# Recurrent steps on single buffers, with two fewer streamed weight blocks and a new order of the matmul units

## The chip, the cores and the metric

The kernel runs on one core of a Trainium2 chip. The metric is the time of the whole kernel on the device, in microseconds, as the median of three runs. The profile is one further execution, taken by the hardware profiler.

## The reference

Two branches work on the same input `x` (2048 tokens of 640 numbers, bf16) and a gate mixes them.

```
g = sigmoid((x * gate_w).sum(-1))          # one number per token
a = sliding-window attention of x          # 32 heads of 20, each token sees the last 256
b = recurrent memory transformer of x      # below
out = g * a + (1 - g) * b

mem = mem0                                 # 8 rows of 640
for s in range(64):                        # segments of 32 tokens
    h = concat(mem, x[32*s : 32*s+32])     # 40 rows
    q, k, v = h @ Wq, h @ Wk, h @ Wv       # 32 heads of 192
    p = softmax(mask(q k^T / sqrt(192)))   # memory rows see all; a token sees no later row
    o = (p v) @ Wo                         # back to 640
    mem = o[:8]; emit o[8:]                # the next step needs these 8 rows
```

The recurrence is strict: step s+1 cannot start its projections before the memory rows of step s exist.

## The kernel before

**Stages.** First comes the sliding-window branch (`branch_A`). Its output, already multiplied by g, is written to `ga_dram`. Then a dense stage computes q, k and v for the last 8 tokens of every segment, all segments at once, since these rows hold no memory. Its results go to the DRAM tensor `xin`, beside the transposed input of each segment. Then `branch_B` runs the 64 recurrent steps on the other 32 rows (8 memory rows and 24 tokens); most of the time is spent there.

**One step.** The 32 heads are worked on in 4 groups g of 8. Each step is a list of units for TensorE (PE), written out by hand in `STEP`, and the same list is issued for every step:

- `k`, `q`, `v` followed by g: a projection of the group, 20 matmuls over 5 slices of the 640 inputs (L772). ScalarE (ACT) copies the result out of PSUM into `tok` or `vtok` (L783).
- `tk`, `tq`: the transposes of k and q (L796). VectorE (DVE) writes k into the buffers `K02` (shown as `b_K`, L819) and `Kz` (L823), ACT writes q into `QT` (L805). GpSimd (POOL) adds the precomputed columns of the 8 last tokens from the tile `xg` (L828, L830 twice, L809; four copies, called xb below), and then issues the DMA that loads the next `xg` (L725).
- `s`: the scores (L843, L850). The softmax runs on DVE and ACT (L861 to L884).
- `p`, then `pv`: the probabilities transposed (L902, L904) and spread by DVE (L916, L911), then times v (L932) and times the precomputed v rows `xv` (L939). ACT copies the result into `OT` (L943).
- `o`: the output projection of the group, 24 matmuls (L963), added up over the four groups in one PSUM bank.
- `m`: after `o3`, DVE copies the step's output to `osum` (L972), PE turns the memory rows (L984), and DVE copies them into the next step's input `hT` (L989). The rest of `hT` was loaded from `xin` by a DMA on POOL's queue (L710).

The end of a step also mixes the branches: POOL stores `osum` to `b_dram` (L994, two DMAs), loads the step's rows of `ga_dram` into the tile `ga` (L995, two DMAs), DVE computes ga + (1 - g) * osum (L998), and POOL stores that to the output (L1002, two DMAs).

**Weights.** The four weight matrices do not fit in SBUF. They are cut into 84 blocks; those named in `STREAMED` are loaded anew in every step into a ring of six buffers `b_w`, by DMAs on SyncE's (SP) queue (L517, L521), each as soon as a ring buffer is free. The others stay in SBUF.

**What sets the order.** Only PE's order is written by hand. `Sched` takes the units with durations, simulates the engines with its own table of latencies, and issues the instructions of DVE, ACT, POOL and SP in the order in which that simulation starts them. Every engine then works strictly in its issued order, and an instruction that has to wait holds up those behind it. `Sched` knows how many buffers each kind of tile has, and an instruction that writes a buffer waits for all users of its former content. `KEPT` and the table `sb` in `branch_B` hold these numbers.

Of the kernel before, what the change touches and what calls it, by code (L numbers as in the profile page):

```python
# [14 lines left out]
SEG = 32  # L15
MEM = 8
# [382 lines left out]
class Sched:  # L399

    LAT = {"PE": 190, "DVE": 125, "ACT": 140, "POOL": 150, "DMA": 5000, "SP": 2500}
    SWITCH = 100

# [8 lines left out]
    def op(self, eng, dur, fn, reads=(), writes=(), after=(), name=None, mode=None):  # L417
        o = dict(eng=eng, dur=dur, fn=fn, n=len(self.ops), deps=set(), outs=[], name=name, mode=mode)
# [17 lines left out]
    def run(self, names=None, emit=True):  # L436
        ops = self.ops
        if names is not None:
            named = {o["name"]: o for o in ops if o["eng"] == "PE"}
            assert len(named) == len(names) == sum(o["eng"] == "PE" for o in ops)  # L440
            names = [named[n] for n in names]
# [4 lines left out]
        for o in reversed(ops):  # L446
            tail = max((ops[k]["rank"] for k in o["outs"]), default=0)
            o["rank"] = o["dur"] + self.LAT[o["eng"]] + tail
        left = {o["n"]: len(o["deps"]) for o in ops}
        free, ready, at, mode = {}, {}, {}, None  # L450

        def enter(o):
            o["by"] = max(o["deps"], key=lambda d: at[d] + ops[d]["dur"] + self.LAT[ops[d]["eng"]], default=None)
            at[o["n"]] = 0 if o["by"] is None else at[o["by"]] + ops[o["by"]]["dur"] + self.LAT[ops[o["by"]]["eng"]]
            ready.setdefault(o["eng"], []).append(o)
# [4 lines left out]
        order, k = [], 0  # L460
        while any(ready.values()):
            best = None
            for eng, rs in ready.items():
                if eng == "PE" and names is not None:
                    rs = [o for o in rs if o is names[k]] if k < len(names) else []
                if not rs:
                    continue
                t0 = max(free.get(eng, 0), min(at[o["n"]] for o in rs))
                if best is None or t0 < best[0]:
                    best = (t0, eng)  # L470
            assert best is not None, ("stuck", names[k]["name"], [(ops[d]["name"], ops[d]["eng"]) for d in names[k]["deps"] if not ops[d].get("done")])
            t0, eng = best
            if eng == "PE" and names is not None:
                o = names[k]
                k += 1
            else:
                o = max((o for o in ready[eng] if at[o["n"]] <= t0), key=lambda o: o["rank"])
            ready[eng].remove(o)
# [4 lines left out]
            o["ready"], o["done"] = at[o["n"]], True  # L483
            at[o["n"]] = o["t"] = t0
            free[eng] = t0 + o["dur"] if eng != "DMA" else 0
# [5 lines left out]
        assert len(order) == len(ops)  # L491
        order.sort(key=lambda x: x[:2])
        if emit:
            for _, _, o in order:
                o["fn"]()
        return max(t + o["dur"] for t, _, o in order)
# [112 lines left out]
def pe_order(nseg):  # L609
# [5 lines left out]
STEP = "k0 q0 k1 tk0 tq0 q1 k2 tq1 s0 tk1 k3 q2 s1 tk2 v0 q3 tq2 p0 v1 tk3 pv0 tq3 s2 v2 p1 s3 o0 pv1 p2 v3 pv2 p3 o1 pv3 o2 o3 m"  # L615


KEPT = {"QT": (2, [P, 12 * L + 64 - L]), "Kz": (2, [P, 4, 2, L]), "Px": (2, [P, 64]), "PTx0": (1, [P, 2, 4, 2, MEM]), "PTx1": (1, [P, 2, 4, 2, MEM]),
        "OT": (2, [P, 12 * L + 64 - L]), "osum": (1, [P, D // 2]), "ga": (1, [P, D // 2])}
# [50 lines left out]
def branch_B(ctx, tc, xin, mem0, weights, ring, c, omg_sb, ga_dram, b_dram, outf, hold, held):  # L670
# [7 lines left out]
        "w": (RING, [P, PIECE]), "tok": (3, [P, 384]), "vtok": (2, [P, 384]), "K02": (2, [P, 4, 2, L]),  # L678
        "PTm": (1, [P, 2, 4, L]), "Pm": (2, [P, 4, SEG]),
        "xg": (2, [P, 2, 12, MEM]), "xv": (1, [P, 384]), "hT": (2, [P, KT, SEG]),  # L680
# [19 lines left out]
    def dve(n):  # L700
        return 75 + n / 0.96

    def act(n):
        return 60 + n / 1.2

    def load_x(s):
        hb = sc.buf("hT")

        def f():
            nc.gpsimd.dma_start(tile_of(hb)[:].rearrange("p k t -> p (k t)"), xin[s, :, 0:KT * SEG])  # L710
        return hb, sc.op("DMA", 500, f, writes=[hb])

    def load_tail(s):
        xv = sc.buf("xv")
        sc.op("DMA", 500, lambda: nc.gpsimd.dma_start(tile_of(xv)[:], xin[s, :, KT * SEG + 768:XIN]), writes=[xv])
        return xv
# [3 lines left out]
    def tail_qk(s, g):  # L720

        if (s, g) not in groups:
            b = groups[s, g] = sc.buf("xg")
            c = KT * SEG + g * 192
            sc.op("DMA", 500, lambda: nc.gpsimd.dma_start(tile_of(b)[:].rearrange("p i b t -> p (i b t)"), xin[s, :, c:c + 192]), writes=[b])  # L725
        return groups[s, g]

    def pieces(kind, g):

        out = {}  # L730
        for m in range(6 if kind == "o" else 5):
            u = (kind, g, m)
            if u in weights.streamed:
                b = out[m] = sc.buf("w")
                sc.op("SP", 0.65 * weights.width(kind), lambda b=b, u=u: weights.load(u, tile_of(b)[:, 0:weights.width(u[0])], nc.sync), writes=[b])
# [6 lines left out]
    for i, u in enumerate(held):  # L742
        b = slow[u] = sc.buf("rest")

        def f_rest(i=i, u=u):
            weights.load_held(hold, i, u, nc.sync)
        sc.op("SP", 0.65 * 2 * D, f_rest, writes=[b])
# [3 lines left out]
    sc.op("DMA", 500, lambda: nc.sync.dma_start(tile_of(m0)[0:MEM, 0:D], mem0), writes=[m0])  # L751
# [6 lines left out]
    sc.op("PE", 300, f_m0, reads=[m0], writes=[tp], name=("m0", 0), mode=128)  # L758
    sc.op("DVE", dve(40), lambda: nc.vector.tensor_copy(tile_of(hts[0][0])[:, :, 0:MEM], tp["tile"][:]), reads=[tp],
# [3 lines left out]
    def chunk(kind, s, g):  # L763
        hT = hts[s][0]
# [9 lines left out]
        for kt in range(KT):  # L774
            sc.op("PE", 160, lambda kt=kt: f(kt), reads=[hT] + [wb[m] for m in wb if m == kt], writes=[b], name=(kind, s, g, kt), mode=32)
# [8 lines left out]
        sc.op("ACT", act(384), ev, reads=[b], writes=[tok])  # L784
        made[kind, s, g] = tok

    def turn(kind, s, g):
# [9 lines left out]
        sc.op("PE", 180, f, reads=[tok], writes=[b], name=("t" + kind, s, g), mode=64)  # L797
        return b

    def turn_q(s, g):  # L800
# [9 lines left out]
        sc.op("ACT", act(384), ev_q, reads=[tq], writes=[QT])  # L810
        sc.op("POOL", 250, xb_q, reads=[xg], writes=[QT])
        made["Q", s, g] = QT

    def turn_k(s, g):
# [16 lines left out]
        sc.op("DVE", dve(256), ev_k, reads=[tk], writes=[K02])  # L831
        sc.op("DVE", dve(256), ev_z, reads=[tk], writes=[Kz])
        sc.op("POOL", 650, xb_k, reads=[xg], writes=[K02, Kz])
        made["K", s, g] = (K02, Kz)

    def scores(s, g):
# [16 lines left out]
        o = sc.op("PE", 330, f, reads=[QT, K02, Kz], writes=[S], name=("s", s, g), mode=64)  # L853
# [21 lines left out]
        for eng, dur, f in (("DVE", dve(160), f1), ("DVE", dve(160), f2), ("ACT", act(160), f3), ("DVE", dve(160), f4), ("DVE", dve(4), f5)):  # L875
            o = sc.op(eng, dur, f, reads=[S], after=[o])
# [9 lines left out]
        sc.op("DVE", dve(128), f6, reads=[S], writes=[Pm], after=[o])  # L886
        sc.op("DVE", dve(32), f7, reads=[S], writes=[Px], after=[o])
# [312 lines left out]
```

## Time and profile before

| What | Value |
|---|---|
| Three runs | 2139.73, 2140.41 and 2146.31 us, median 2140.41 us |
| The profiled execution | 2141.04 us, of which its span in the profile is 2139.3 us |
| Recurrent steps | the copies into `hT` (L989) run from 464.4 us to 2105.8 us: 62 intervals, 26.47 us a step |
| PE busy over the span | 1943.8 us (91%) |
| DVE, ACT, POOL busy | 1027.0, 914.1, 717.9 us |
| Weights streamed in a step | 24 blocks: 14 of 384 KB and 10 of 320 KB |
| Granted clock of PE, mean | 0.991 |

A line of instructions in the profile gives the start, the duration, the engine, the line of the kernel and the tiles; in square brackets stands the idle time of the engine just before, and what ended it. A line on a DMA gives the median time from issue to landing.

### The profile page before, as it was taken

The page shows a single profiled execution, that of the slowest core. Times are in us where ns is not written, and L with a number is a line of the kernel's source. Part 1 is how long each engine was busy: PE and PEld are TensorE (multiplying, and loading weights), DVE is VectorE, ACT ScalarE, POOL GpSimd, SP SyncE. Part 2 cuts the span into 40 slices and gives each one's busy share as a digit, 9 for nine tenths or more (in the row PEclk, how much of TensorE's full clock was granted, in tenths as well). Part 3 has the DMA queues.
Part 4 walks back from the last instruction along what each step waited for, and adds up shares of the span by engine and source line. Part 5 has one row for each costly group of instructions (what it writes and reads, how often), then busy time and mean ns, then how long its engine had stood idle before and what let it go on. Part 6 is the DMA issues. An engine that isn't in the chain of part 4 may idle for free. (4 is left out here: it accounts for less than half of the span.)

```text
span 2139.3 us, 92706 instructions
## 1 busy us (share of the span) xinstructions
PE 1943.8 (91%) x39670; PEld 1442.4 (67%) x39670; DVE 1027.0 (48%) x3338; ACT 914.1 (43%) x1885; POOL 717.9 (34%) x2011
## 2 busy tenths in 40 slices
PE   7999999989988899899889998899899899888997
PEld 6878788656666666666666666666666666666665
DVE  4888843344444444444444444444444444444444
ACT  3888823234433334343334433443333443343343
POOL 4211121343333333333333333333333333333332
PEclk9999999999999999999999999999999999999999
DMA  4322168799999999999999999999999999999997
GB/s 133 88 77 82 33 176 283 217 326 363 363 351 340 345 358 355 330 346 351 346 343 350 355 350 344 350 367 362 351 360 360 360 355 350 353 350 349 348 367 273
DMA packets 278374, 655.81 MB, mean 307 GB/s; under 512 B 42552, under 2 KB 62144, under 8 KB 277952
## 3 DMA queue, kind: packets, MB, share of 16 engines
q1 hardware_dynamic: 246464, 602.01, 78.5%
q0 software_dynamic: 31488, 47.78, 7.6%
q8 instruction: 313, 5.13, 0.9%
q14 instruction: 109, 0.89, 0.1%
HBM read 620.26 MB, written 29.37 MB: 304 GB/s over the span
## 5 line engine op out<-in xcount | busy, mean ns | idle before, releaser
L772 PEld LDWEIGHTS <-b_hT 128*32 128x32 bf16 x15360 | 379.5, 96 | 302.3 <-issue 101.7
L963 PEld LDWEIGHTS <-b_OT 128*64 128x64 bf16 x6144 | 399.7, 110 | 69.1 <-issue 63.5
L963 PE MATMUL ps_o<-b_w,b_OT 128*64 128x320 bf16 x2560 | 300.3, 303 | 39.4 <-DMA b_w<-in_B_Wo_dram 32.4
L783 ACT CAST b_tok<-ps_k 128x384 bf16<-128x384 f32 x256 | 122.5, 478 | 435.1 <-PE ps_k L772 435.0
L772 PE MATMUL ps_k<-w_k,b_hT 128*32 128x384 bf16 x4096 | 247.4, 330 | 19.0 <-DVE b_hT L989 18.7
L963 PE MATMUL ps_o<-hold,b_OT 128*64 128x320 bf16 x2560 | 235.9, 299 | 0.4 <-DMA hold<-in_B_Wo_dram 0.4
L772 PE MATMUL ps_q<-w_q,b_hT 128*32 128x384 bf16 x3840 | 235.6, 329 | 0.0
L772 PE MATMUL ps_v<-w_v,b_hT 128*32 128x384 bf16 x3840 | 229.8, 329 | 4.8 <-issue 4.7
L943 ACT CAST b_OT<-ps_pv 128x480 bf16<-128x480 f32 x256 | 142.9, 558 | 167.2 <-PE ps_pv L939 115.2
L819 DVE COPY b_K<-tr_k 128x256 bf16<-128x256 bf16 x256 | 73.1, 286 | 287.6 <-PE tr_k L796 279.3
L239 ACT ACTIVATE pt<-s_ps 128x1024 bf16<-128x1024 f32 x180 | 183.5, 1025 | 55.2 <-PE s_ps L236 52.0
L783 ACT CAST b_vtok<-ps_v 128x384 bf16<-128x384 f32 x256 | 122.8, 480 | 166.2 <-PE ps_v L772 165.6
L972 DVE CAST b_osum<-ps_o 128x320 bf16<-128x320 f32 x64 | 31.4, 491 | 336.4 <-PE ps_o L963 336.4
L783 ACT CAST b_tok<-ps_q 128x384 bf16<-128x384 f32 x256 | 122.4, 478 | 111.4 <-PE ps_q L772 110.9
L725 POOL DMA_DIRECT2D b_xg<-xin x256 | 139.5, 545 | 84.7 <-POOL b_QT L809 55.9
L796 PEld LDWEIGHTS <-b_tok 128*64 128x64 bf16 x3072 | 100.4, 110 | 83.5 <-issue 35.8
L861 DVE TENSOR_REDUCE sm<-S_ps 128x4 f32<-128x160 f32 x256 | 81.9, 320 | 154.6 <-PE S_ps L850 147.4
L995 POOL DMA_DIRECT2D b_ga<-ga_dram x128 | 63.5, 497 | 263.3 <-DMA out_dram<-b_ga 257.8
L994 POOL DMA_DIRECT2D b_dram<-b_osum x128 | 64.1, 506 | 260.6 <-DVE b_osum L972 254.2
L916 DVE TENSOR_TENSOR b_PTm<-PT_ps,mk_m 128x320 bf16<-128x320 f32 x256 | 123.3, 482 | 49.3 <-PE PT_ps L904 48.0
L828 POOL COPY b_K<-b_xg 128x64 bf16<-128x64 bf16 x256 | 61.5, 240 | 253.2 <-PE S_ps L850 162.7
L867 ACT ACTIVATE S_ps<-S_ps 128x160 f32<-128x160 f32 x256 | 74.5, 291 | 143.4 <-DVE S_ps L864 139.1
(142 smaller groups left out, 3853.4 us busy)
## 6 DMA issues: line engine op xcount, KB each, us to landing
b_w<-in_B_Wo_dram SPq DMA_DIRECT2D x640, 320.0 KB, 5.1
b_w<-in_B_Wq_dram SPq DMA_DIRECT2D x320, 384.0 KB, 5.8
b_w<-in_B_Wv_dram SPq DMA_DIRECT2D x320, 384.0 KB, 5.4
b_w<-in_B_Wk_dram SPq DMA_DIRECT2D x256, 384.0 KB, 5.7
xin<-hold POOLq DMA_DIRECT2D x8, 1536.0 KB, 12.5
b_xg<-xin POOLq DMA_DIRECT2D x256, 48.0 KB, 4.9
w_k<-in_B_Wk_dram SPq DMA_DIRECT2D x16, 384.0 KB, 3.4
b_xv<-xin POOLq DMA_DIRECT2D x64, 96.0 KB, 5.7
```

Of the source, the lines that this page charges most:

```text
L239: nc.scalar.activation(out=pt, in_=sp[:], func=ACT.Exp, scale=scale)
L725: sc.op("DMA", 500, lambda: nc.gpsimd.dma_start(tile_of(b)[:].rearrange("p i b t -> p (i b t)"), xin[s, :, c:c + 192]), writes=[b])
L772: nc.tensor.matmul(t[32 * j:32 * j + 32, 0:384], lhsT=tile_of(hT)[:, kt, :], rhs=w[:, j * 384:(j + 1) * 384], start=(kt == 0), stop=(kt == ...
L783: nc.scalar.copy(dst, src)
L796: nc.tensor.transpose(t[64 * a:64 * a + 64, k, :], tok["tile"][:, c:c + 64], ident[:], tile_position=(0, 64 * a))
L819: nc.vector.tensor_copy(tile_of(K02)[:, :, :, 0:SEG], src)
L861: nc.vector.tensor_reduce(out=x["mx"][:], in_=view(), axis=AX.X, op=ALU.max)
L867: nc.scalar.activation(out=view(), in_=view(), func=ACT.Exp, scale=scale)
L916: nc.vector.tensor_tensor(out=tile_of(PTm)[:], in0=src.to_broadcast([P, 2, 4, L]), in1=mk_m[:].unsqueeze(1).unsqueeze(3).to_broadcast([P, ...
L943: sc.op("ACT", act(480), lambda: nc.scalar.copy(tile_of(OT)[:, 0:12 * L], o["tile"][:, 0:12 * L]), reads=[o], writes=[OT])
L963: nc.tensor.matmul(t[64 * h:64 * h + 64, 0:D // 2], lhsT=OT["tile"][:, c:c + 64], rhs=w, start=(g == 0 and m == 0 and n == 0), stop=(g == ...
L994: sc.op("DMA", 500, lambda h=h: nc.gpsimd.dma_start(half(b_dram, h), mine(osum["tile"], h)), reads=[osum])
```

## The change

It does four things.

1. `QT`, `Kz`, `OT`, `K02`, `Pm`, `xg` and `hT` go from two buffers to one; `vtok` too, and it moves from a pool to the fixed tiles of `KEPT`. `Px` stays at two.
2. `osum` and `ga` lose their own tiles. The step output takes the one buffer of `OT`, the mix takes the one buffer of `vtok`.
3. `STREAMED` names 22 blocks instead of 24: one block of Wq and one of Wv fewer, and other blocks in part. The blocks that stay are placed in SBUF, some of them loaded during the first step.
4. `Sched` gets other durations and latencies, models SP as one queue with a server, and counts POOL's DMA issues as POOL's work. `STEP` has a new order, and the load of the next `hT` is entered after the twelfth projection of a step and no longer at its start.

```diff
-STEP = "k0 q0 k1 tk0 tq0 q1 k2 tq1 s0 tk1 k3 q2 s1 tk2 v0 q3 tq2 p0 v1 tk3 pv0 tq3 s2 v2 p1 s3 o0 pv1 p2 v3 pv2 p3 o1 pv3 o2 o3 m"
+STEP = "k0 q0 q1 tk0 tq0 k1 s0 tq1 k2 v0 tk1 q2 p0 s1 tk2 q3 tq2 pv0 k3 v1 p1 s2 tk3 o0 tq3 pv1 v2 p2 s3 o1 pv2 v3 p3 o2 pv3 o3 m"
-KEPT = {"QT": (2, ...), "Kz": (2, ...), "Px": (2, [P, 64]), "PTx0": (1, ...), "PTx1": (1, ...),
-        "OT": (2, ...), "osum": (1, [P, D // 2]), "ga": (1, [P, D // 2])}
+KEPT = {"QT": (1, ...), "Kz": (1, ...), "Px": (2, [P, 64]), "PTx0": (1, ...), "PTx1": (1, ...),
+        "OT": (1, ...), "vtok": (1, [P, 384])}
...
-        "w": (RING, [P, PIECE]), "tok": (3, [P, 384]), "vtok": (2, [P, 384]), "K02": (2, [P, 4, 2, L]),
-        "PTm": (1, [P, 2, 4, L]), "Pm": (2, [P, 4, SEG]),
-        "xg": (2, [P, 2, 12, MEM]), "xv": (1, [P, 384]), "hT": (2, [P, KT, SEG]),
+        "w": (RING, [P, PIECE]), "tok": (3, [P, 384]), "K02": (1, [P, 4, 2, L]),
+        "PTm": (1, [P, 2, 4, L]), "Pm": (1, [P, 4, SEG]),
+        "xg": (1, [P, 2, 12, MEM]), "xv": (1, [P, 384]), "hT": (1, [P, KT, SEG]),
...
-        osum = sc.buf("osum")
+        osum = sc.buf("OT")
...
-        ga, rows = sc.buf("ga"), slice(s * SEG, (s + 1) * SEG)
+        ga, rows = sc.buf("vtok"), slice(s * SEG, (s + 1) * SEG)
...
         if s not in tails:
-            tails[s] = load_tail(s)
-            if s + 1 < nseg:
-                hts[s + 1] = load_x(s + 1)
+            tails[s], left = load_tail(s), 12
         if kind == "m":
             finish(s)
         elif kind in "qkv":
             chunk(kind, s, n[2])
+            left -= 1
+            if not left and s + 1 < nseg:
+                hts[s + 1] = load_x(s + 1)
...
-LAST = 10
+LAST = 11
...
-STREAMED = {"q": ((2, 4), (), (1, 4), (1,)),
-            "k": ((3,), (3,), (3,), (0,)),
-            "v": ((0,), (2, 3), (1,), (4,)),
-            "o": ((0, 3, 5), (0, 3, 5), (0, 5), (3, 5))}
+STREAMED = {"q": ((), (4,), (2, 4), (3,)),
+            "k": ((0, 4), (4,), (), (3,)),
+            "v": ((2,), (4,), (0,), (0,)),
+            "o": ((0, 3, 5), (0, 3), (2, 5), (0, 3, 5))}
...
-    LAT = {"PE": 190, "DVE": 125, "ACT": 140, "POOL": 150, "DMA": 5000, "SP": 2500}
     SWITCH = 100
+    SAME = 20
+    ISSUE, BEFORE, AFTER = 60, 1300, 1000
...
-            sc.op("DMA", 500, lambda h=h: nc.gpsimd.dma_start(mine(tile_of(ga), h), half(ga_dram, h)), writes=[ga])
+            sc.op("POOL", 500, 2500, lambda h=h: nc.gpsimd.dma_start(mine(tile_of(ga), h), half(ga_dram, h)), writes=[ga])
```

POOL's issued order within one step, for the changed kernel, as its instructions stand in the built program:

```
xb(1) load xg(2) | xb(2) load xg(3) | xb(3) load xg(0, next) | xb(0, next) load xg(1, next)
load hT(next) | load ga, load ga | load xv | store b_dram x2 | store out x2
```

The waits that stand in that program: xb(g) waits for the landing of xg(g) and for the score matmuls of the group before it; a load of `xg` waits for the xb that read the former content; the loads of `ga` wait for `pv3`'s matmuls on `vtok`; the mix on DVE (L998 before, L1001 after) stands ahead of the copy into `hT` (L989 before, L991 after) in DVE's order and waits for both loads of `ga`. Before the change the mix stands ahead of that copy too. Line numbers in what follows are those of the kernel before unless said otherwise; the changed file is two to three lines longer there.

## The prediction

> **What bounds the kernel now.** I read the page first, then the busy time by stage, PE's waits, the DMA list, and last the timeline of POOL and DVE in a step at 1010 to 1030 us. The stages show that the steps keep the DMA engines full (columns: length; busy us and instructions of PE, PEld, DVE, ACT, POOL; clock; DMA share; GB/s):
>
> ```profile
> 1000.00:1500.00 500.00, 452.31 (x9962) 327.40 (x9958) 224.77 (x817) 198.88 (x455) 181.53 (x530) 0.99 0.99 353
> ```
>
> PE's waits (us in total, times, longest) say what that costs. The four streamed weights sum to 75.1 us over 64 steps, 1.17 us a step. The end of a step costs 56.1 us more.
>
> ```profile
> PE mem_ps L984 <- DVE b_osum L972: 37.4, 64, 0.6
> PE ps_o L963 <- DMA b_w<-in_B_Wo_dram: 32.4, 57, 2.1
> PE ps_v L772 <- DMA b_w<-in_B_Wv_dram: 20.4, 48, 2.4
> PE ps_k L772 <- DVE b_hT L989: 18.7, 63, 0.3
> PE ps_q L772 <- DMA b_w<-in_B_Wq_dram: 15.2, 28, 1.5
> ...
> PE ps_k L772 <- DMA b_w<-in_B_Wk_dram: 7.1, 15, 1.1
> ```
>
> So a step of 26.47 us is PE work with 1.17 us of weight waits in it. Nothing of POOL stands in this list: its loads run one or two buffers ahead. How long they take is in the DMA list, and this decides the change:
>
> ```profile
> b_xg<-xin POOLq DMA_DIRECT2D x256, 48.0 KB, 4.9
> b_ga<-ga_dram POOLq DMA_DIRECT2D x128, 20.0 KB, 4.7
> ```
>
> **What the change takes away.** The streamed bytes fall from 8576 to 7808 KB a step (14 and 12 blocks of 384 KB, ten of 320 KB). With the 448 KB of small transfers that is 8256 against 9024 KB, 0.915. The DMA engines were busy for 0.985 of 26.47 us, 26.1 us; they now need 23.9. By that alone the weight waits go, at most 1.17 us a step. What is late next?
>
> **What it adds on PE.** `pv3` now stands right before `o3`, and `OT` has one buffer. In the timeline `pv` starts at 1018.27, its last matmul ends at 1018.77, ACT's copy runs from 1018.86 to 1019.42; `o3` could start 1.2 us after `pv3`, where it now starts after 0.3. That is 0.9 us a step. PE alone then gives 26.47 - 1.17 + 0.9 = 26.2 us. The other reorderings of `STEP` I cost at nothing: between `s` and its `p` stand at least 2.9 us of PE work (s3 to p3: o1, pv2, v3), and the softmax takes about 2.4 (its seven rows sum to 1.9, the rest is hand-over).
>
> **What it adds on POOL: a closed loop.** With two buffers of `xg`, a load has two groups of time. With one, the load for g+1 is issued when xb(g) is done, and xb(g+1) waits for its landing. One xb and its load, from POOL's timeline:
>
> ```profile
> 1013.47 0.25 POOL L828 COPY b_K<-b_xg 128x64 bf16<-128x64 bf16 x1
> 1013.64 0.48 POOL L830 COPY b_Kz<-b_xg 64x32 bf16<-64x32 bf16 x2
> 1014.18 0.26 POOL L809 COPY b_QT<-b_xg 128x96 bf16<-128x96 bf16 x1
> 1014.74 0.54 POOL L725 DMA_DIRECT2D b_xg<-xin  x1 [0.30 <-POOL b_QT L809]
> ```
>
> From the first copy to the issue pass 1.27 us; a landing is followed by the copy after 0.15 us (landing times against starts in the trace). Behind xb(0, next) POOL's order holds, one after the other, the load of `xg`, that of `hT` and the two of `ga`. So `ga` is queued behind a landing that it has nothing to do with. The mix waits for `ga`, the copy into `hT` stands behind the mix on DVE, and k0 waits for that copy:
>
> ```profile
> 1022.57 0.49 DVE L972 CAST b_osum<-ps_o 128x320 bf16<-128x320 f32 x1 [5.51 <-PE ps_o L963]
> 1023.10 0.55 DVE L998 SCALAR_TENSOR_TENSOR b_ga<-b_osum,omg_sb,b_ga 128x320 bf16<-128x320 bf16 x1
> 1023.70 0.20 DVE L989 CAST b_hT<-mem_ps 128x40 bf16<-128x40 f32 x1
> ```
>
> Before, `ga` has a tile of its own and is loaded from 1029.04 us for a mix a whole step after 1023.10; the mix runs while PE works on `m`. Now the loop is closed from k0 to k0. With D for the time from issue to landing:
>
> - mix start to k0: 0.85 (1023.10 to 1023.95, k0's first matmul).
> - k0, q0, q1, k1: 4 x 0.83 (q1 at 1027.01, k2 at 1027.84) = 3.32; tk0 and tq0 0.45 (1026.56 to 1027.01); two changes of tile shape, 0.12 each (1015.54 to 1015.66); s0 until its last matmul ends, 0.48 (1010.50 to 1010.98). Together 4.49.
> - xb(1) and its issue: 1.27, then D.
> - xb(2), xb(3), xb(0, next), each 0.15 + 1.27; a D after each of the first two.
> - the issues of `xg` 0.545, `hT` 0.535 and the first `ga` 0.497, 1.58 in all; then D of the second `ga`, and 0.05.
>
> The fixed part is 0.85 + 4.49 + 1.27 + 3 x 1.42 + 1.58 + 0.05 = 12.5 us, and D comes in four times. The loop takes 12.5 + 4D. PE's 26.2 us decide only below D = 3.4.
>
> **How large D is.** At today's load it is 4.85 (three of 4.9, one of 4.7). The lightest stretches in the steps are two in which PE was slow. Around 665 us the DMA share is 0.71, and the loads landed after 3.2 us:
>
> ```profile
> q1 hardware_dynamic: 587, 1.34, 69.6%
> b_xg<-xin POOLq DMA_DIRECT2D x1, 48.0 KB, 3.2
> b_hT<-xin POOLq DMA_DIRECT2D x1, 40.0 KB, 3.2
> ```
>
> From 902.49 to 909.32 us the share is 0.68, and two `xg` landed after a median of 3.9. I take the middle, 3.5 at 0.70, and 4.85 at 0.99, and a straight line between: 4.66 us per unit of share. A step of P us has a share of 23.9 / P. At P = 30.0 that is 0.797, and D = 3.5 + 0.097 x 4.66 = 3.95.
>
> The Trainium skill ("DMA: Bandwidth & Descriptors", section "Anatomy of one DMA — SWDGE (gpsimd) path") gives about 2.0 us plus bytes / 436e3 for such a load, 2.1 us for `xg`, by which the loop would be an estimated 20.9 us and never decide. No row here is that short, and the rows are used.
>
> **PE's clock.** In the loop PE idles between `m` and k0. From the load behind xb(3), `ga` lands after 3.95 + 1.42 + 1.58 + 3.95 = 10.9, and k0 starts at 11.8. PE, released at the same time, is done with `m` after 8.9: s3 0.5, three `o` at 1.63 (24 matmuls, four in 0.27), v3 0.93, pv2 and p3 0.45, pv3 until o3 1.2, the step's output 0.65, `m` 0.3. That is an idle stretch of up to 3 us in every step. Such stretches have a row now:
>
> ```profile
> 660.15:663.56 3.41, 1.20 (x43) 0.71 (x32) 1.40 (x5) 0.94 (x3) 1.17 (x5) 1.00 0.99 368
> 663.56:666.97 3.41, 3.41 (x36) 2.34 (x34) 1.48 (x7) 0.29 (x1) 1.39 (x5) 0.50 0.71 217
> 666.97:670.38 3.41, 3.41 (x75) 2.89 (x73) 1.96 (x6) 1.53 (x3) 0.53 (x1) 1.00 0.83 240
> ```
>
> PE was busy for 1.20 of 3.41 us, and the next 3.41 us ran at clock 0.50 with 36 matmuls where 75 follow. A stretch at half clock loses 1.7 us, and after the idle end of a step it falls on k0 to s0, inside the loop. I add 1.7; the bounds are 0 and 3.4 (902.49 to 909.32 is two such stretches).
>
> The Trainium skill ("TensorE: Matmul & The Clock Gate", section "Part 1: The HAM clock gate") asks for an idle window of about 3.4 us before the clock falls. Read strictly it would spare this gap, and the estimate would be 28.9 us a step; the rows show a fall with 1.20 us of work in the window.
>
> **The sum.** P = 12.5 + 4 x 3.95 + 1.7 = 30.0 us, 3.53 more than 26.47. It is paid at 63 starts of a step: 222 us. The first stage changes by one or two block loads and one more block in step 0, under 2 us, not counted. The profiled execution took 2141.04 us (span 2139.3), 0.6 above the median: 2141 + 222 = 2363 us.
>
> **The rivals.** Two differ in one term:
>
> - *The clock holds.* At 1837.75 us PE is busy for 1.67 of 3.41 us and no fall follows. Without the 1.7, P = 12.5 + 4D with D = 4.1 is 28.9 us: 2141 + 63 x 2.43 = 2294 us. Chance 0.18.
> - *D does not fall with the load*, since the loads meet the bursts after o2 and o3. P = 12.5 + 19.4 + 1.7 = 33.6: 2590 us. Chance 0.10.
> - *Faster: PE stays the bound.* If D is 3.2 throughout, as at 663 us, the loop is 25.3 us and hides behind PE's 26.2: 2141 - 63 x 0.27 = 2124 us. It decides below D = 3.4 with the clock held. For it speak the freed 8.5% of the bytes; against it, 23.9 us of transfers in 26.2 are 0.91, where the line gives D = 4.5. Chance 0.05.
> - Between these, P of 26.4 to 27.6: 0.05, of which 0.02 within the noise.
>
> **How the numbers follow.** The main case has 0.62. A measurement here can tell about 0.3% from no change, 6 us. Faster 0.05, same 0.02, slower 0.93. The range runs from P = 27.6 (D = 3.8 with the clock held) to 32.2 (D = 4.5 with 1.7, or about 3.95 with 3.4 of clock): 2141 + 63 x 1.13 = 2212 and 2141 + 63 x 5.73 = 2502. The faster, the equal and the fully loaded case lie outside.
>
> **What would show it.** Right: k0's wait for `b_hT` grows from 0.3 to 2 us or more per step; DVE idles before the mix, ended by the landing of `b_ga`; POOL idles before L830 (new lines), ended by `b_xg`; the steps' DMA share is near 0.80, D near 4, the clock below 0.95. Wrong: `b_xg` at 3.3 us and PE's busy share above 0.9, or weight waits still on top of PE's list.

## The result, and the profile after

The changed kernel takes 2472.93 us (median of four runs, 2468.31 to 2478.82); the kernel before takes 2142.80 us (median of four). The ratio is 1.154, 95% interval 1.151 to 1.158. The forecast was 2363 us with a range of 2212 to 2502: the direction and the mechanism held, the size came out a third too small (+222 us forecast, +330 us measured).

The profiled execution took 2471.93 us, its span is 2470.0 us. The copies into `hT` (L991 now) run from 474.2 to 2435.4 us: 62 intervals of 31.63 us, where 26.47 was the time before and 30.0 the forecast.

The steps, by stage (columns as in the prediction: length; busy us of PE, PEld, DVE, ACT, POOL; clock; DMA share; GB/s):

```profile
1000.00:1500.00 500.00, 398.86 (x8307) 273.44 (x8307) 191.15 (x680) 167.71 (x378) 153.79 (x443) 0.91 0.84 271
```

PE's busy time fell from 452 to 399 of 500 us, its clock from 0.99 to 0.91, and the transfers no longer fill the step. What PE waits for (us in total, times, longest):

```profile
PE ps_k L774 <- DVE b_hT L991: 271.9, 63, 6.5
PE ps_o L965 <- ACT b_OT L945: 45.0, 64, 0.7
PE mem_ps L986 <- DVE b_OT L974: 41.2, 64, 0.7
...
PE ps_v L774 <- DMA b_w<-in_B_Wv_dram: 5.1, 4, 2.7
```

The weight waits are all but gone, in a step that is also 5 us longer. In their place k0 waits for the copy into `hT`: 18.7 us before, 271.9 us now, 4.3 us in each step. The waits of the other engines say what stands behind that copy:

```profile
POOL b_K L830 <- PE S_ps L852: 337.0, 64, 6.1
POOL b_K L830 <- DMA b_xg<-xin: 326.5, 83, 5.6
...
DVE b_vtok L1001 <- DMA b_vtok<-ga_dram: 264.7, 64, 6.4
```

The first row is the start of the loop, xb(1) behind s0. The second is POOL waiting for the landings of `xg`; in the trace nearly every xb(2), xb(3) and xb(0, next) begins 0.15 us after its landing, also where the list names another engine. 264.7 us of DVE's idle time stand ahead of the mix (L1001, which now writes the tile `vtok`) and were ended by the landing of `ga`; nearly the same sum appears at k0, because the copy into `hT` is the next instruction on DVE. One step's end shows the queue, first POOL, then DVE, then PE (start, duration, engine, line, tiles; idle time before it):

```profile
1512.41 0.24 POOL L830 COPY b_K<-b_xg 128x64 bf16<-128x64 bf16 x1 [3.39 <-PE PT_ps L906]
...
1513.67 0.54 POOL L719 DMA_DIRECT2D b_xg<-xin  x1 [0.29 <-POOL b_QT L811]
1514.21 0.54 POOL L704 DMA_DIRECT2D b_hT<-xin  x1
1514.74 1.00 POOL L997 DMA_DIRECT2D b_vtok<-ga_dram  x2
```

```profile
1519.91 0.55 DVE L1001 SCALAR_TENSOR_TENSOR b_vtok<-b_OT,omg_sb,b_vtok 128x320 bf16<-128x320 bf16 x1 [2.57 <-DMA b_vtok<-ga_dram]
1520.38 0.19 DVE L991 CAST b_hT<-mem_ps 128x40 bf16<-128x40 f32 x1
```

```profile
1517.40 0.54 PE L986 MATMUL mem_ps<-ident,b_OT 128*64 128x8 bf16 x10 [0.64 <-DVE b_OT L974]
1520.62 0.51 PE L774 MATMUL ps_k<-b_w,b_hT 128*32 128x384 bf16 x4 [2.69 <-DVE b_hT L991]
```

xb(0, next) begins at 1512.41: the load of `xg` issued at 1508.48 landed at 1512.26 by the trace (the bracket names a PE instruction that ended within 0.05 us of it). Behind it POOL issues `xg`, `hT` and `ga`; `ga` lands, the mix runs, the copy follows, and k0 starts at 1520.62, though the memory rows had been ready since about 1518. The clock answers to the gap (same columns as above):

```profile
1512.00:1515.50 3.50, 2.80 (x51) 2.56 (x49) 0.79 (x2) 1.04 (x2) 2.68 (x8) 1.00 1.04 363
1515.50:1519.00 3.50, 1.80 (x30) 1.25 (x24) 0.49 (x1) 0.00 (x0) 1.81 (x4) 1.00 0.96 330
1519.00:1522.50 3.50, 1.88 (x24) 0.94 (x28) 0.66 (x2) 0.03 (x1) 0.99 (x2) 0.51 0.91 319
1522.50:1526.00 3.50, 3.50 (x52) 1.73 (x44) 0.00 (x0) 1.26 (x3) 0.00 (x0) 0.52 0.73 221
```

After a stretch with 1.80 us of work in 3.5, PE runs at half clock from 1519.05 us for 6.83 us, over k0, q0 and q1 of the new step; k1 starts at 1526.14, at full clock again. There are 63 stretches at half clock in the steps, about one a step, 6.0 us long on average.

### The profile page after: what moved, and what is told of

It reads as the page before. It is cut to its first block, busy times and chain, and to the rows that moved or that the text cites. A ratio compares the mean times of both kernels' runs of the same rounds, so it can differ in the third digit from the quotient of the medians.

```text
span 2470.0 us, 92645 instructions
## 1 busy us (share of the span) xinstructions
PE 2031.6 (82%) x39670; PEld 1439.0 (58%) x39670; DVE 1045.3 (42%) x3338; ACT 924.3 (37%) x1885; POOL 721.9 (29%) x2007
## 3 DMA queue, kind: packets, MB, share of 16 engines
q1 hardware_dynamic: 228032, 551.67, 67.4%
## 4 chain that ended last, share of the span: by engine, by line
PE 49%; DMA 26%; POOL 8%; issue 7%; DVE 6%; ACT 3%; POOLq 0%; DVEq 0%; SPq 0%; ACTq 0%
DMA b_vtok<-ga_dram 13%; DMA b_xg<-xin 12%; PE ps_q L774 11%; PE ps_k L774 9%; PE ps_o L965 6%; PE ps_v L774 4%; PE t_psum L584 3%; PE qk_ps L138 3%; POOL b_Kz L832 2%; PE tr_k L798 2%; PE S_ps L852 2%; PE tr_q L798 2%; PE s_ps L236 1%; POOL b_QT L811 1%; POOL b_vtok L997 1%
## 5 line engine op out<-in xcount | busy, mean ns | idle before, releaser
L774 PEld LDWEIGHTS <-b_hT 128*32 128x32 bf16 x15360 | 402.6, 106 | 549.8 <-DVE b_hT L991 277.5
L965 PEld LDWEIGHTS <-b_OT 128*64 128x64 bf16 x6144 | 357.7, 110 | 87.7 <-ACT b_OT L945 52.1
L830 POOL COPY b_K<-b_xg 128x64 bf16<-128x64 bf16 x256 | 60.1, 235 | 1034.6 <-PE S_ps L852 337.0
L774 PE MATMUL ps_k<-b_w,b_hT 128*32 128x384 bf16 x1024 | 108.0, 412 | 277.1 <-DVE b_hT L991 271.9
L965 PE MATMUL ps_o<-b_w,b_OT 128*64 128x320 bf16 x2560 | 289.6, 301 | 46.6 <-ACT b_OT L945 45.0
L774 PE MATMUL ps_q<-w_q,b_hT 128*32 128x384 bf16 x4096 | 295.6, 417 | 0.0
L825 DVE TENSOR_TENSOR b_Kz<-tr_k,mk_z 128x256 bf16<-128x256 bf16 x256 | 106.0, 414 | 326.6 <-PE tr_k L798 326.6
L774 PE MATMUL ps_v<-w_v,b_hT 128*32 128x384 bf16 x4096 | 221.3, 326 | 0.0
L945 ACT CAST b_OT<-ps_pv 128x480 bf16<-128x480 f32 x256 | 143.4, 560 | 147.4 <-PE ps_pv L941 143.9
L798 PEld LDWEIGHTS <-b_tok 128*64 128x64 bf16 x3072 | 112.2, 113 | 71.5 <-issue 41.8
L1001 DVE SCALAR_TENSOR_TENSOR b_vtok<-b_OT,omg_sb,b_vtok 128x320 bf16<-128x320 bf16 x64 | 35.3, 552 | 264.7 <-DMA b_vtok<-ga_dram 264.7
L807 ACT COPY b_QT<-tr_q 128x384 bf16<-128x384 bf16 x256 | 122.9, 480 | 64.6 <-PE tr_q L798 56.2
```

Source lines behind the costliest of these rows:

```text
L774: nc.tensor.matmul(t[32 * j:32 * j + 32, 0:384], lhsT=tile_of(hT)[:, kt, :], rhs=w[:, j * 384:(j + 1) * 384], start=(kt == 0), stop=(kt == ...
L798: nc.tensor.transpose(t[64 * a:64 * a + 64, k, :], tok["tile"][:, c:c + 64], ident[:], tile_position=(0, 64 * a))
L807: nc.scalar.copy(dst, tq["tile"][:].rearrange("p b (j t) -> p b j t", t=SEG))
L825: nc.vector.tensor_tensor(out=tile_of(Kz)[:, :, :, 0:SEG], in0=src, in1=mk_z[:].unsqueeze(1).unsqueeze(3).to_broadcast([P, 4, 2, SEG]), op ...
L945: sc.op("ACT", 560, 50, lambda: nc.scalar.copy(tile_of(OT)[:, 0:12 * L], o["tile"][:, 0:12 * L]), reads=[o], writes=[OT])
L965: nc.tensor.matmul(t[64 * h:64 * h + 64, 0:D // 2], lhsT=OT["tile"][:, c:c + 64], rhs=w, start=(g == 0 and m == 0 and n == 0), stop=(g == ...
```

## The experiments

Theory A, the prediction's: a loop closes from k0 through POOL's queue. Each of xg(2), xg(3), xg(0, next) and `ga` is issued only after the landing before it, and the mix and the copy into `hT` wait at the loop's end. Its rivals, lettered anew in each expectation: one shared tile or one missing buffer is the cause by itself; the number of buffers counts and not the order; the transfers are the bound. The first five kernels each cut or cheapen one link of the loop; one run each, against effects of 100 us and more.

**The second buffer of `xg` back** (`e1_xg2`), on the changed kernel:

```diff
-        "xg": (1, [P, 2, 12, MEM]), ...
+        "xg": (2, [P, 2, 12, MEM]), ...
```

> The changed kernel with one edit: xg has two buffers again. Theory A (the closed loop on POOL's queue: three landings of xg and one of ga in every step, plus the half clock): the landings of xg leave the loop, ga stays in it behind pv3. A step is then PE's k0 to pv3, about 21.5 us, plus 0.4 + 0.3 + 0.5 + 5.0 + 0.85 us for ga and the mix, plus about 1.5 us of half clock: about 29.8 us instead of 31.6, some 2360 us (2300 to 2430). Rival B (the single xg buffer alone is the cause): back to PE's bound of 26.2 us a step, about 2130 us. Rival C (the mix in front of the copy into hT alone): no change, 2473 us.

Measured: 2331.52 us, 29.5 us a step, k0's wait 168.1 us, DMA share 0.88, clock 0.91 in the steps. A is right to 30 us. The landings of `xg` have left the loop. What is left runs through `pv3`: its matmuls read the tile that the mix shares, POOL can issue the loads of `ga` only behind them, and their landing, the mix and the copy into `hT` follow.

```profile
POOL b_vtok L997 <- PE ps_pv L941: 106.5, 61, 3.1
```

**The copy into `hT` ahead of the mix on DVE** (`e2_ht_first`):

```diff
-            sc.op("DVE", 200, 55, lambda: ...copy into hT..., reads=[b], writes=[hT], after=[xl])
+            turned = sc.op("DVE", 200, 55, lambda: ...copy into hT..., reads=[b], writes=[hT], after=[xl])
...
-        sc.op("DVE", 552, 60, f_r, reads=[osum], writes=[ga])
+        sc.op("DVE", 552, 60, f_r, reads=[osum], writes=[ga], after=[turned])
```

> The changed kernel with one edit: the mix waits for the copy into hT, so DVE turns the memory rows first and the landing of ga no longer holds up k0. Theory A: the loop then closes through the load of hT, which stands on POOL behind xb(0, next): 0.25 + 4.5 + 1.3 + 3.5 + 1.4 + 4.2 + 1.4 + 4.5 + 1.4 + 0.55 + 4.8 + 0.3 = 28.1 us, plus about 1.2 us of half clock: 29.3 us a step, about 2330 us (2270 to 2400). Rival B (the xg buffer alone): no change, 2473 us. Rival C (the mix in front of the copy alone): PE's bound, about 2130 us.

Measured: 2305.26 us, k0's wait 143.9 us. `ga` is off the path by the order of two DVE instructions alone, and this returns 168 us. What is late next is the load of `hT`, which still stands behind xb(0, next).

**A tile of its own for `ga`** (`e5_ga_own`):

```diff
-        ga, rows = sc.buf("vtok"), slice(s * SEG, (s + 1) * SEG)
+        ga, rows = sc.buf("ga"), slice(s * SEG, (s + 1) * SEG)
```

> The changed kernel, but the mix has a tile of its own again (320 columns, as before) and no longer shares the one of v. The planner then issues the two loads of ga right after the stores of the mix before, a whole step early, so the mix waits for no landing. Theory A (a closed loop through POOL's queue, in which whatever tile stands last ends it): the load of hT still stands behind xb(0, next), so the copy into hT now waits for that landing. The end of the loop, 1.69 from the issue of xg(1, next) to that of the second ga, 5.03 of landing, 0.12 and 0.71 until k0, becomes 0.55 until hT's issue, about 4.8 of landing, 0.1 and 0.25 until k0: 5.7 instead of 7.55 us. 1.85 us less a step, 63 times: about 2355 us (2320 to 2390). k0 keeps waiting for b_hT, 2 to 4 us a step, but DVE's idle time before the copy into hT is now ended by the landing of b_hT. Theory B (the mix's shared tile is the cause by itself): PE's bound returns, 2110 to 2150 us. Theory C (it is not the cause at all): 2473 us.

Measured: 2330.84 us, 29.4 us a step. DVE's idle time ahead of the copy into `hT` is now ended by the landing of `hT` (125.4 us), as forecast. The three links are worth 141, 168 and 142 us alone, 451 together, more than the 330 that the whole change costs: whichever is taken away, another landing ends the loop, that of `ga` behind `pv3` or that of `hT` behind xb(0, next). No single one of them is the cause.

**Work for PE in the gap** (`e3_fill`):

```diff
+            if kind == "k" and g == 0 and kt == 0 and s:
+                for i in range(FILL):                     # FILL = 18
+                    nc.tensor.matmul(t[0:32, 0:384], lhsT=ident[:, 0:32], rhs=weights.tiles["q", 0, 0][:, 0:384], start=True, stop=True, ...)
```

> The changed kernel with 18 matmuls of 128x32 by 384 added on PE between m and k0 (about 2.9 us at full clock, results overwritten by k0), to keep PE busy while it waits for the copy into hT. Theory A: the clock stays near full, k0 to the end of s0 falls from 6.4 to about 4.6 us, and a step by about 1.8 us: about 2360 us (2330 to 2400). Rival (the clock lies beside the loop): 2473 us within 10, at a higher clock.

Measured: 2371.34 us, mean clock 0.987, 30.05 us a step; 9 half-clock stretches are left in the steps. k0 still comes when the copy into `hT` comes, and the kernel is 102 us faster with more work on PE. k0 to the end of s0 takes 4.75 us on average, 6.40 without the added matmuls. So the half clock there costs 1.6 us a step.

**Half the bytes** (`e4_half`):

```diff
+        if half:
+            n = self.width(kind) // 2
+            c = g * PIECE if kind != "o" else 0
+            src = self.W[kind][:, m, c:c + n] if kind != "o" else self.Wo[:, 4 * g, 0:n]
+            engine.dma_start(dst[:, 0:n], src)
+            return
```

> The changed kernel with the streamed weight DMAs bringing only the first half of each block (the matmuls read that half twice, so the weights are wrong in part; the number of matmuls is unchanged). Theory A with landing times that follow the load on the DMA engines: the landings in the loop fall from 3.5, 4.2, 4.5 and 5.0 us to about 3.2 to 3.4 each, 4 us less in sum: a step of 27.6 us, about 2220 us (2170 to 2290). Rival (the landing times are fixed costs of these loads, or the loop is not what binds): 2473 us within 20.

Measured: 2121.76 us, below the expected range. The stage and the loads:

```profile
1000.00:1500.00 500.00, 453.36 (x10284) 325.66 (x10278) 237.35 (x846) 208.53 (x472) 188.81 (x547) 1.00 0.62 176
```

```profile
b_xg<-xin POOLq DMA_DIRECT2D x256, 48.0 KB, 2.8
```

`xg` and `ga` are as large as before; only what streams beside them shrank. The four landings of the loop sum to 11.2 us (2.54, 2.92, 3.05, 2.70) in place of 17.2. By them the loop falls to some 24 us, below PE's own time, and the step is 26.1 us. k0 still waits 52.4 us for the copy in all; ahead of the loads of `ga`, POOL now mostly waits for `pv3` (78.4 us, 47 times). The miss was in the floor set for D, 3.2 us. D falls with the load, and the rival in which it doesn't is out.

**Order alone** (`e6_queue`): all single buffers stay. As in `e2_ht_first`, and on POOL xb(0, next) and its load of `xg` go behind the load of `hT`, in the built order also behind those of `ga` and `xv`:

```diff
-        sc.op("POOL", 660, 60, xb_k, reads=[xg], writes=[K02, Kz])
+        sc.op("POOL", 660, 60, xb_k, reads=[xg], writes=[K02, Kz], after=[hts[s][1]] if g == 0 else ())
...
-        sc.op("POOL", 263, 60, xb_q, reads=[xg], writes=[QT])
+        sc.op("POOL", 263, 60, xb_q, reads=[xg], writes=[QT], after=[hts[s][1]] if g == 0 else ())
```

> The changed kernel with all its single buffers; two dependences are added that only move instructions. On DVE the copy into hT goes ahead of the mix; on POOL xb(0, next) and the load of xg(1, next) go behind the loads of hT, ga and xv, so the load of hT is issued as soon as v3 has read the old one. The same matmuls, bytes, buffers and blocks. Theory A (the time is in the order of the queues, not in the number of buffers as such): the loop through a step is cut. xg has 4 x (1.42 + D) = 23.7 us with D of 4.5, hT is issued behind v3 and lands some 5 us later, while PE has about 6.3 us of work until the copy. PE's own 26.2 us decide: 2124 us (2105 to 2185; the upper end where the one xg still costs 1 us a step). k0's wait for b_hT is below 1 us a step. Theory B (single buffers cost whatever the order is): between 2250 and 2473 us. Theory C (the transfers bound it, since the DMA engines are busy for 26.4 us in each step of the changed kernel): 2140 us, DMA share above 0.97 and weight waits on PE.

Measured: 2172.73 us, 1.013 of the kernel before (1.010 to 1.017). Two dependences return 300 of the 330 us, with every buffer single and the same bytes, and the time lies in A's range. PE's waits:

```profile
PE S_ps L852 <- POOL b_QT L811: 59.8, 55, 2.3
PE ps_o L965 <- ACT b_OT L945: 45.0, 64, 0.7
...
PE ps_k L774 <- DVE b_hT L991: 18.6, 63, 0.3
```

k0's wait is what it was before the change. What is left is the single `xg`: 0.95 us a step, at which the scores wait for xb.

**With the second buffer of `xg`, and with `pv3` covered** (`e9_queue_xg2`, `e7_order_and_ot`). The first adds the edit of `e1_xg2` to `e6_queue`. The second also puts group 3's attention output elsewhere and issues the last three pieces of o2 behind pv3:

```diff
-        OT = sc.buf("OT")
+        OT = sc.buf("QT" if g == 3 else "OT")
...
+            if n[0] == "o" and n[2] == 2:
+                late += [n + (m,) for m in range(3)]
+            elif n[0] == "pv" and n[2] == 3:
+                late += [n] + [("o", n[1], 2, m) for m in range(3, 6)]
```

> As the kernel with the two added dependences, and two things more: xg has its two buffers back, and the wait between pv3 and o3 is covered. Group 3's attention output goes to the buffer of QT, which is free by then, and the last three sixths of o2 are issued behind pv3. The same matmuls and bytes. Theory A: no loop through POOL is left; PE's own time decides, 26.2 us less the 0.7 us that PE waited in each step for the copy of pv3 (and less at most 0.1 for the pass into the next step): 25.5 us a step. 2141 - 63 x 0.97 = 2080 us (2060 to 2110), faster than both kernels. Theory C (the transfers need 26.4 us a step, as the busy time of the DMA engines in the changed kernel has it): no gain beyond 2130 to 2145 us, DMA share above 0.98, and weight waits on PE again. If instead the share is about 23.9 / 25.5 = 0.94 and the weight waits stay below 0.3 us a step, the 26.4 us were no need of the transfers.

> As the kernel with the two added dependences (2172.7 us), and xg has its two buffers back; group 3's attention output stays in OT, and o2 is whole. It splits the 92 us between that kernel and the one with all three things (2081.1 us) into the part of xg and that of the wait between pv3 and o3. Theory A: the 41.5 us that PE waited for ACT's copy stay, the 55.6 us that the scores waited for POOL go: 2172.7 - 55.6 = 2117 us, up to 2130 if weight waits come back (the kernel with all three has 24 us of them). Rival: the wait for POOL is only replaced by waits for weights, and the 92 us are mostly those of pv3: 2150 us or more.

Measured: 2086.43 us for the first (0.973 of the kernel before, 0.970 to 0.976), 2081.09 us for the second (0.970, 0.967 to 0.973). Both beat both kernels. Nearly all of the 92 us came from `xg`: in the order of `e6_queue` its second buffer is worth 86 us. The second kernel met its forecast, but by the wrong sum: it removed the 43.6 us of waits between pv3 and o3, and the step is 25.5 us in both profiled executions (that of the first was the fastest of its five, 2077.74 us). The two lists show how (first `e9_queue_xg2`, then `e7_order_and_ot`):

```profile
PE ps_o L965 <- ACT b_OT L945: 43.6, 62, 0.7
PE mem_ps L986 <- DVE b_OT L974: 41.2, 64, 0.7
PE ps_k L774 <- DVE b_hT L991: 18.8, 63, 0.4
PE ps_v L774 <- DMA b_w<-in_B_Wv_dram: 8.0, 11, 2.3
PE ps_o L965 <- DMA b_w<-in_B_Wo_dram: 7.5, 14, 1.2
```

```profile
PE mem_ps L986 <- DVE b_OT L974: 41.0, 64, 0.7
PE ps_k L774 <- DVE b_hT L991: 19.7, 62, 0.7
PE ps_o L965 <- DMA b_w<-in_B_Wo_dram: 12.2, 24, 1.3
PE ps_v L774 <- DMA b_w<-in_B_Wv_dram: 10.9, 14, 1.9
```

The weight waits of these rows rise by 7.6 us, PE's idle time falls by 16 us only (170.6 to 154.4 us), and its busy time over the span rises from 1905.3 to 1925.0 us, part of it by a clock of 0.990 against 0.997 in the two profiled executions. Why the rest of the 43.6 us did not come out is open. The DMA share of the second is 0.96 at 25.5 us a step, 24.5 us of busy engines: the transfers need no 26.4 us, and its theory C is out.

**One part of the change alone** (`e8_before_xg1`): the kernel before with one `xg`.

> The kernel before with one part of the change alone: xg has one buffer and not two. Its ga, hT, osum and all other buffers stay, 24 streamed blocks. Theory A: the loop of xg by itself is 4 x (1.42 + D); with D of 4.85 at the full load of this kernel that is 25.1 us, still 1.4 us below the step of 26.47, and the load of hT and the six transfers of the mix are issued while a load of xg is in flight. So little is lost: 2141 to 2185 us (some meetings of a late landing with s). Theory B (one buffer of xg is what costs the changed kernel its time): half or more of the 330 us, above 2300 us. Theory C (no price at all): 2141 us within 0.3%.

Measured: 2267.85 us, 1.056 of the kernel before (1.052 to 1.060); neither A nor B. POOL at a step's end (1024 to 1033 us, that kernel's lines):

```profile
1024.29 0.55 POOL L725 DMA_DIRECT2D b_xg<-xin  x1 [0.30 <-POOL b_QT L809]
1029.29 0.54 POOL L710 DMA_DIRECT2D b_hT<-xin  x1 [4.46 <-PE ps_v L772]
1029.83 0.25 POOL L828 COPY b_K<-b_xg 128x64 bf16<-128x64 bf16 x1
...
1031.70 0.55 POOL L715 DMA_DIRECT2D b_xv<-xin  x1 [1.22 <-PE ps_o L963]
1032.29 0.26 POOL L809 COPY b_QT<-b_xg 128x96 bf16<-128x96 bf16 x1
1032.85 0.54 POOL L725 DMA_DIRECT2D b_xg<-xin  x1 [0.30 <-POOL b_QT L809]
```

The passes of the loop, from one first copy to the next (1010.32, 1016.61, 1023.03, 1029.83, 1038.44), take 6.3, 6.4, 6.8 and 8.6 us. The first two are the 1.42 + 4.85 expected. The last two hold the loads of `hT` and `xv`, which wait for PE; together the four are 28.1 us, and the step is 28.6. This is not the order of the kernel before. There the four xb of a step, each with its load, follow one another on POOL, the loads of `hT` and `xv`, the stores and the loads of `ga` stand behind them, and POOL is not among PE's waits. With one buffer `Sched` made another order, and in it the hold-up is added to the loop. Three more kernels move these instructions out, one kind after another: the loads of `hT` and `xv` (`e10_before_xg1_free`), then the four stores (`e11_before_xg1_free2`), then the loads of `ga` (`e12_before_xg1_free3`). Their edits give the instruction a dependence on an earlier xb, and enter the loads of `hT` and `xv` at the first scores of a step:

```diff
-            tails[s] = load_tail(s)
+            tails[s] = load_tail(s, xbs[-2:])
...
-                hts[s + 1] = load_x(s + 1)
+                hts[s + 1] = load_x(s + 1, xbs[-2:])
...
-            sc.op("DMA", 500, lambda h=h: nc.gpsimd.dma_start(half(b_dram, h), mine(osum["tile"], h)), reads=[osum])
+            stores.append(lambda x, h=h: sc.op("DMA", 500, lambda: nc.gpsimd.dma_start(half(b_dram, h), mine(osum["tile"], h)), reads=[osum], after=x))
...
-            sc.op("DMA", 500, lambda h=h: nc.gpsimd.dma_start(mine(tile_of(ga), h), half(ga_dram, h)), writes=[ga])
+            sc.op("DMA", 500, lambda h=h: nc.gpsimd.dma_start(mine(tile_of(ga), h), half(ga_dram, h)), writes=[ga], after=behind[s])
```

> The kernel before with one xg, as in the run that took 2268 us where about 2160 was expected, but the loads of hT and xv are issued behind xb(0) of the step and no longer stand between the load of xg(0, next) and that of xg(1, next) in POOL's order. Buffers, bytes and matmuls are the same. Theory A (the miss came from that order: the loop of xg is 25.1 us only if nothing in POOL's queue makes it wait for PE; in that run the load of hT waited for v3 and the load of xv for the end of pv3, and the last copy of xb(0) and the load of xg(1) behind them): 2141 to 2170 us, and the scores' wait for POOL on PE falls from 106 us to below 30. Theory B (one xg by itself costs the 120 us, since its landings at this load are too late for the scores): 2250 us or more, with the same waits.

> As the run before it (the kernel before with one xg, the loads of hT and xv behind xb(0): 2219 us), and the stores of the step output and of the mix are issued behind xb(0, next) as well. In that run they took the place of the two loads: POOL waited for the step output until 1020.56 us, so that xb(0, next) came at 1022.53 and the load of xg(1, next) at 1023.80, where the load of xg(0, next), issued at 1014.85, had landed about 4.9 us later; 2.8 us late in that step. Theory A (only the waits in POOL's queue make one xg dear): 2145 to 2185 us, the scores' wait for POOL below 30 us. Theory B (one xg costs what is left, since its landings are late at this load): 2200 us or more with the same 61 us of waits, or waits of the xb copies for landings that grow as the others go.

> As the run before it (2274 us), and the two loads of ga are issued behind xb(2). In the trace of that run they had become the new stop: they wait for the landing of the store of the mix, 5.1 us of idle POOL until 1020.55, and xb(2) behind them came at 1021.55, though the load issued at 1011.83 had landed some 4.8 us later; the other passes of xb took 6.3, 4.1 and 5.7 us. (The names of groups in the last two expectations are one too low there: the copies of q for the next group are made ahead of s0, so the loads and stores went behind xb(1), and it was xb(1, next) that came late in the run before.) Nothing that waits for PE's end of step or for a store now stands between a landing and its xb. Theory A (a single xg costs only what POOL's queue makes it wait; its loop is 4 x 6.3 = 25.2 us): 2141 to 2175 us, and the scores' wait for POOL falls from 102 us to below 30. Theory B (the landings at this load make one xg dear whatever the order): 2215 us or more.

Measured: 2219.23 us (1.034, 1.030 to 1.038), 2274.32 us (1.062, 1.056 to 1.067) and 2168.08 us (1.009, 1.007 to 1.012). The first two missed, by the same thing each time: what was moved left the loop, and another waiting instruction came to stand in it. By its time alone `e11_before_xg1_free2` would speak for theory B; the traces say what stood there. In `e10_before_xg1_free` it was the store to `b_dram`, which waits for the step's output (336.8 us of idle POOL, 163.9 in `e8_before_xg1`). In `e11_before_xg1_free2` it was `ga`, which waits for a store to land:

```profile
1011.83 0.54 POOL L725 DMA_DIRECT2D b_xg<-xin  x1 [0.31 <-POOL b_QT L809]
...
1020.55 1.01 POOL L995 DMA_DIRECT2D b_ga<-ga_dram  x2 [5.08 <-DMA out_dram<-b_ga]
1021.55 0.25 POOL L828 COPY b_K<-b_xg 128x64 bf16<-128x64 bf16 x1
```

When nothing of the kind is left, the scores' wait for POOL falls from 102.0 to 5.8 us (in `e8_before_xg1` it was 106.4):

```profile
PE S_ps L852 <- POOL b_QT L809: 5.8, 5, 2.2
```

So in the kernel before one `xg` alone costs 1% in the last of these orders and 6% in the one that `Sched` made for it. In the changed kernel, in the order of `e6_queue`, it costs 4% (2172.73 against 2086.43 us): the price is a matter of order, but no order tried here brings it to nothing.

## Why the prediction was right, and where its size was off

- **Transfers.** Weight waits were said to go, and they went (5.1 us in the rows above), in a step that is 5 us longer; at 25.5 us a step, in `e9_queue_xg2`, 15.9 of the 75.1 us are left. But the busy time of the engines was said to fall to 23.9 us a step; it is 0.84 of 31.63, 26.6 us. This step of the working failed; why the engines were busy for longer is open.
- **PE alone.** pv3 to o3 was put at 0.9 us and measured 45.0 / 64 = 0.70. The whole bound of 26.2 us was too high: 25.5 in `e9_queue_xg2`, with that wait still in it. PE's busy time there is 1905.3 against 1943.8 us before, 0.6 us a step that the sum did not have, in part by the clock of that execution (0.997 against 0.991); `e6_queue`, at 0.992, has 1924.9 us, 0.3 us a step. The reorderings of `STEP`, put at nothing because 2.9 us of PE work cover a softmax of 2.4, do show once: in the changed kernel PE waits 24.5 us for the softmax ahead of p1, 0.4 us a step. That wait lies off the loop, and `e9_queue_xg2` does not have it.
- **The loop, fixed part.** Mix to k0 0.71 (0.85 forecast), each xb with its issue 1.27 and a landing to its copy 0.15 (as forecast), the issues until the second `ga` 1.69 (1.58), its landing to the mix 0.12 (0.05). k0 to the end of s0 took 6.40 where 4.49 plus the clock's 1.7 was forecast, 6.19. Together 14.5 against 14.2.
- **The clock.** 1.7 us was right as a number: 1.9 from 6.40 - 4.49, and 1.6 by `e3_fill`. The rival in which the clock holds is out. That it fits is partly luck: the stretches are nearly twice as long as assumed (6.0 against 3.41 us), but part of each falls on time in which PE waits anyway. The Trainium skill ("TensorE: Matmul & The Clock Gate", section "Part 1: The HAM clock gate") asks for an idle window of about 3.4 us; the row of 1515.50 to 1519.00 has PE busy for 1.80 of 3.50 us and the clock falls all the same. Over the 63 falls PE was busy for 0 to 1.90 us of the 3.41 us before, 0.73 in the median. The measurement decides.
- **D, the mis-sized term.** Four landings were put at 4 x 3.95 = 15.8 us. They measured 3.52, 4.16, 4.50 and 5.03, 17.2 us: 1.4 of the 1.63 us by which the step was longer than forecast. About half of that comes from the share: the straight line was entered at 0.797, by the failed step on the transfers, and at the 0.84 that was measured it gives 4.15, against a mean of 4.30. The rest is that the load that ended the loop, `ga`, was the slowest of the four. That the line comes so near is partly luck, for other kernels lie off it: `e6_queue` has 4.2 us for `xg` at a share of 0.94, where it gives 4.62, and `e1_xg2` 4.7 at 0.88, where it gives 4.34.
- **The sum.** 63 x (31.63 - 26.47) = 325 us and some 5 us more in the first step and the end explain the 330. By the formula of the Trainium skill ("DMA: Bandwidth & Descriptors", section "Anatomy of one DMA — SWDGE (gpsimd) path") D would be an estimated 2.1 us and the loop 20.9. The trace agrees only where little else moves: the `xg` load issued at 440.25 us, at the start of the steps of the changed kernel, landed after 2.0 us, with a DMA share of 0.12 over these 2.2 us. In the steps the lowest median of `xg` is 2.8 us, in `e4_half`, and the measurement decides.
- **The signs named in advance** all came: k0's wait for `b_hT` 4.3 us a step, DVE ended by `ga`, POOL ended by `b_xg` before L830, `b_xg` at 4.1 us, clock below 0.95. The share is 0.84 where 0.80 was named.
- **The faster case**, with D low enough for PE to be the bound, came only in `e4_half`, where half the streamed bytes were gone.

## What to carry to other kernels

Before a double buffer is taken away, list what stands in the issuing engine's queue between the landing of one load and the issue of the next: each landing and each wait for another engine in that list becomes a term of a loop, and the loop is compared with the step. The cost lies in the order as much as in the buffers: with the same single buffers the changed kernel is 330 us slower than the kernel before in one order and some 30 in another, where a second `xg` would still return 86. A planner that makes the order anew from its own latencies can put a waiting instruction into that list, as `Sched` did in `e8_before_xg1`; the trace shows it. Removing one wait shows only its distance to the next one, so the gains of single repairs do not add up.

## What the runs showed of the hardware

- **The busy time of the DMA engines was no measure of what the transfers need.** The packets of the streamed weights (packets, MB, share of 16 engines' span) in the changed kernel, and below in `e7_order_and_ot`, which moves the same bytes:

```profile
q1 hardware_dynamic: 228032, 551.67, 67.4%
```

```profile
q1 hardware_dynamic: 228032, 551.67, 75.3%
```

  0.674 x 16 x 2470.0 us / 228032 is 117 ns a packet, 0.753 x 16 x 2079.4 / 228032 is 110 ns; before it was 109. The same packets took 6% longer in the kernel that moved them more slowly. Why is open.
- **The landing time of a small load depends on what streams beside it:** a 48 KB load took 4.9 us at a DMA share of 0.99 and 0.96, 4.1 at 0.84 and 2.8 at 0.62 with half the streamed bytes (medians). The mean share does not settle it: in `e6_queue` it was 4.2 at 0.94, in `e1_xg2` 4.7 at 0.88. What else counts is not shown.
- **Work without use can save time:** 18 matmuls in the gap at a step's end made the changed kernel 102 us faster, since only 9 half-clock stretches were left where there had been about one a step.
